# Counting some of a search's bounds on ScalarE with sums of signs, and one search no longer on TensorE

## The chip, the cores and the metric

The kernel runs on one core of a Trainium2 chip. The metric is the device time of one execution in microseconds (us), the median of several runs. Before the change it is 3851.02 us, the median of 3 runs from 3850.89 to 3852.55.

The engines of a core run side by side, each with its own instructions in order: TensorE (PE: matmuls; PEld: its weight loads), VectorE (DVE), ScalarE (ACT), GpSimd (POOL) and SyncE (SP), which here only issues transfers.

## The reference

The input is 8 sequences of 3072 tokens with 256 numbers each. Three parts follow each other.

1. The real part of a Fourier transform over the sequence and over the 256 numbers gives 24576 tokens of 256 numbers.
2. A layer of 8 experts. Each token has one score per expert (`x @ w_gate`). All 196608 pairs of token and expert are taken in order of falling score. A pair is skipped when its token already has an expert, or when its expert is full: each takes exactly 24576 / 8 = 3072 tokens. Then every token goes through its expert, `relu(x @ w1[e]) @ w2[e]`, with 1024 numbers in the middle.
3. A layer for all tokens, `h = x @ w_in` (2048 numbers), `g = max(h, 0) + alpha * min(h, 0)`, and `g @ w_out`.

## The kernel before

**Stages.** `fft_phase` computes the transform with matmuls and the scores `LG` (to about 410 us); `Router.first` finds the first expert that fills up and the list of its tokens, while TensorE has little else to do (to about 450 us). From there `ffn_phase` works through 48 tiles of 512 tokens, six tiles for each expert (`TPE`). The order of experts is that in which they fill up, so a next expert and its list have to be found while the tiles of an earlier one are computed.

**A tile.** For a tile `t`, i goes from 0 to 7 and each i has six parts: `l1` (the expert's first layer, six matmuls of 512 columns), `l3` (the first layer of part 3 for tile t-1), `l4` (its second layer, twelve matmuls of 256 columns), `l3`, `l2` (the expert's second layer) and `l4`. All numbers of a product are split into a high and a low half, and three products are summed. After the matmuls of a part are issued, one piece of background work is issued (`next(bg)`), and then the part's `evac()`: for `l1` ScalarE makes `hs` from PSUM and VectorE its low half; for `l3` ScalarE makes `r` and `a`, VectorE combines them, and ScalarE and VectorE make the halves of `g`, one `l3` later. The tiles of PSUM for `l1` and `l3` turn over three buffers.

**The background.** `background()` goes through the experts one after another with `router.round`, where n is the number of experts that are still open: 7, 6, ... 1. Every `yield` ends a piece; `lag()` yields until two further pieces have begun. A round has these steps: `rank` gives each token its best open expert (`aw`, and one-hot masks `ohe`); a search finds the score at which the first of the n experts is full; `choose` and `place` make the list of its tokens, with small matmuls in groups of 16, each after two pieces that VectorE prepares; then scores are moved for the next round. A round r (of 1 to 7) may begin at the tile (r-2)*6, and the list must be there when the last tile of the expert before is at i = 5: where it isn't, the pieces that are left are issued one after another with no layers between them.

**The search.** A token's key has two halves of 16 bits, searched one after the other. With n from 6 to 2, `search()` inside `round` finds 16 bits in 8 steps of 2 bits. `ke` holds the keys, masked for each expert. In each step VectorE counts, for every expert and each of three bounds, how many keys of a row reach the bound: a `tensor_scalar` with `accum_out` (L857). A matmul with ones (`total`, L848) sums the counts over the 128 rows, and VectorE compares the largest with the capacity, subtracts what was found from `ke`, and adds it to `base` (L867 to L874). With n below 6 each expert is a piece, with 6 two experts are; then come two pieces of `lag`, one for the matmul and one for the comparison.

With n = 7 the search is another one, `search_beside`: 4 bits a step, so 4 steps for each half. VectorE writes for each key which of 15 bounds it reaches (L725), and TensorE counts with 24 products a step (L735), 8 at a time, and a sum over the rows (L765). It runs from about 495 to 651 us.

Of the kernel before, what the change touches and what calls it, by code (L numbers as in the profile page):

```python
# [10 lines left out]
F32 = mybir.dt.float32  # L11
F32R = mybir.dt.float32r
BF16 = mybir.dt.bfloat16
I32 = mybir.dt.int32
I16 = mybir.dt.int16
U16 = mybir.dt.uint16
F16 = mybir.dt.float16
AF = mybir.ActivationFunctionType
ALU = mybir.AluOpType
AX = mybir.AxisListType  # L20
# [3 lines left out]
P = 128  # L24
B, N, D = 8, 3072, 256
E = 8
TOK = B * N
N1, N2 = 96, 32
NG = 24
# [239 lines left out]
class Router:  # L269
# [20 lines left out]
    def __init__(self, ctx, tc, LG):  # L290
# [12 lines left out]
        self.ohe = self.oh.rearrange("p a e -> p (a e)").rearrange("p (e a) -> p e a", e=E)  # L303
        self.eid = rp.tile([P, E], F32, name="eid")
        self.wm = rp.tile([P, 1], F32, name="wm")
        self.estar = rp.tile([P, 1], F32, name="estar")
        V.memset(self.done, 0.0)

# [381 lines left out]
                yield  # L690
        yield

    def search_beside(self, psum, n):


        nc, wp, V = self.nc, self.wp, self.nc.vector
        cap = self.CAP - 8 * 1536
        ke = wp.tile([P, E - 1, NCOL], U16, tag="ke", name="lows")
        kf = ke.rearrange("p e a -> p (e a)")
        lows = kf.bitcast(I16)[:, :512].rearrange("p (i k j) -> p i k j", i=4, j=8)  # L700
        dm = kf.bitcast(F32)[:, 256 : 256 + 8 * E].rearrange("p (e c) -> p e c", e=E)
        s2 = kf.bitcast(F16)[:, 640 : 640 + 16 * E].rearrange("p (e k) -> p e k", e=E)
        for i in range(4):
            nc.gpsimd.iota(lows[:, i], pattern=[[1 << 4 * i, 16], [0, 8]], base=-32768, channel_multiplier=0)
        H = NG // 3

        def blocks(t):
            return t.rearrange("p (a b) -> p a b", b=8)

        def search(key, exact=None):  # L710
            for i in reversed(range(4)):
                step = 1 << 4 * i
                last = exact is not None and i == 0
                k = 16 if last else 15
                first = 1 if last else 0
                q = 8 * k
                inds = {}

                def ind(h):
                    t = wp.tile([P, H, 16, 8], BF16, tag="ol", bufs=2, name="ind")  # L720
                    s = slice(h * H, h * H + H)
                    if last:
                        V.tensor_scalar(t[:, :, 0, :], blocks(exact)[:, s], self.base, None, op0=ALU.is_ge)
                    sh = [P, H, k - first, 8]
                    V.tensor_tensor(  # L725
                        t[:, :, first:k], blocks(key)[:, s, None, :].broadcast_to(sh),
                        lows[:, i, None, 16 - k + first :, :].broadcast_to(sh), op=ALU.is_ge,
                    )
                    inds[h] = t

                def products(h):
                    t = inds.pop(h)
                    for c in range(H):
                        a = (h * H + c) * 8
                        nc.tensor.matmul(  # L735
                            dv, t[:, c, :k].rearrange("p k j -> p (k j)"), self.ohe[:, :n, a : a + 8],
                            start=(h + c == 0), stop=(h == 2 and c == H - 1),
                        )

                ind(0)  # L740
                yield
                ind(1)
                yield from self.lag()
                d = psum(name="d")
                dv = d[:q, : 8 * n].rearrange("p (e c) -> p e c", e=n)
                products(0)
                yield
                ind(2)
                products(1)
                yield  # L750
                yield from self.lag()
                products(2)
                yield
                V.tensor_tensor(dm[:q, :n], dv, self.mske[:q, None, :].broadcast_to([q, n, 8]), op=ALU.mult)
                s = wp.tile([P, E], F32, tag="we", name="se")
                V.tensor_reduce(out=s[:q, :n], in_=dm[:q, :n], op=ALU.add, axis=AX.X)

                V.scalar_tensor_tensor(
                    s2[:q, :n, :k], s[:q, :n, None].broadcast_to([q, n, k]), -1536.0,
                    self.mskj[:q, None, :k].broadcast_to([q, n, k]), op0=ALU.add, op1=ALU.mult,  # L760
                )
                yield from self.lag()
                cnt = psum(name="cnt")
                cv = cnt[:, : n * k].rearrange("p (e k) -> p e k", e=n)
                nc.tensor.matmul(cv, self.ones[:q], s2[:q, :n, :k], start=True, stop=True)  # L765
                yield
                if last:
                    return cv
                mc = wp.tile([P, 16], F32, tag="mc", name="mc")
                V.tensor_reduce(out=mc[:, :k], in_=cv.rearrange("p e k -> p k e"), op=ALU.max, axis=AX.X)  # L770
                st = wp.tile([P, 16], F32, tag="st", name="st")
                V.memset(st[:, :k], float(step))
                nk = wp.tile([P, 1], F32, tag="nk", name="nk")
                V.scalar_tensor_tensor(
                    mc[:, :k], mc[:, :k], cap, st[:, :k], op0=ALU.is_ge, op1=ALU.mult, accum_out=nk
                )
                if i:
                    nxt = wp.tile([P, NCOL], I16, tag="cur", bufs=2, name="cur")
                    V.tensor_scalar(nxt, key, nk, -32768.0, op0=ALU.subtract, op1=ALU.max)
                    key = nxt  # L780
                V.tensor_tensor(self.base, self.base, nk, op=ALU.add)
                yield

        k16 = wp.tile([P, NCOL], I16, tag="k16b", name="k16b")
        V.tensor_scalar(k16, self.hi, -32768.0, None, op0=ALU.max)
        V.memset(self.base, -32768.0)
        yield
        yield from search(k16)
        key = self.low_key()
        V.tensor_scalar(k16, key, -32768.0, 32767.0, op0=ALU.max, op1=ALU.min)  # L790
        V.memset(self.base, -32768.0)
        yield
        cv = yield from search(k16, key)

        ce = wp.tile([P, E, 16], F32, tag="q1", name="ce")
        V.tensor_scalar(ce[:, :n], cv, cap, None, op0=ALU.is_ge)
        ne = wp.tile([P, E], F32, tag="ne", name="ne")
        V.tensor_reduce(out=ne[:, :n], in_=ce[:, :n], op=ALU.add, axis=AX.X)
        me = wp.tile([P, 1], F32, tag="me", name="me")
        V.tensor_reduce(out=me, in_=ne[:, :n], op=ALU.max, axis=AX.X)  # L800
        yield
        we = wp.tile([P, E], F32, tag="we", name="we")
        V.scalar_tensor_tensor(we[:, :n], ne[:, :n], me, self.wE[:, :n], op0=ALU.is_equal, op1=ALU.mult)
        V.scalar_tensor_tensor(self.base, me, -1.0, self.base, op0=ALU.add, op1=ALU.add)
        V.tensor_reduce(out=self.wm, in_=we[:, :n], op=ALU.max, axis=AX.X)
        V.scalar_tensor_tensor(
            we[:, :n], we[:, :n], self.wm, self.eid[:, :n], op0=ALU.is_equal, op1=ALU.mult, accum_out=self.estar
        )
        yield
        return key  # L810

    def round(self, psum, lists, n):

        nc, wp = self.nc, self.wp
# [7 lines left out]
            yield from self.place(psum, lists, at, n)  # L822
            return
        yield from self.rank(n)
        if n == E - 1:
            key = yield from self.search_beside(psum, n)
            at = self.choose(key)
            yield "expert"
            yield from self.place(psum, lists, at, n)
            return  # L830
        ke = wp.tile([P, E - 1, NCOL], U16, tag="ke", name="ke")
        s = wp.tile([P, E - 1, 3], BF16, tag="s", name="s")
        junk = [wp.tile([P, NCOL], BF16, tag="w", bufs=2, name="junk") for _ in range(2)]

        def keys(k16):
# [15 lines left out]
        def search():  # L851
            step = 65536
            while step > 1:
                step >>= 2
                for e in range(n):
                    for k in range(3):
                        V.tensor_scalar(  # L857
                            junk[(e + k) % 2], ke[:, e], float((k + 1) * step), 0.0, op0=ALU.is_ge, op1=ALU.add,
                            accum_out=s[:, e, k : k + 1],
                        )  # L860
                    if e % 2 or n < 6:
                        yield
                yield from self.lag()
# [1 line left out]
                yield  # L865
                mc = wp.tile([P, 3], F32, tag="mc", name="mc")
                V.tensor_reduce(out=mc, in_=cv.rearrange("p e k -> p k e"), op=ALU.max, axis=AX.X)  # L867
                st = wp.tile([P, 3], F32, tag="st", name="st")
                V.memset(st, float(step))
                nk = wp.tile([P, 1], F32, tag="nk", name="nk")  # L870
                V.scalar_tensor_tensor(mc, mc, self.CAP, st, op0=ALU.is_ge, op1=ALU.mult, accum_out=nk)
                if step > 1:
                    V.tensor_scalar(ke[:, :n], ke[:, :n], nk, 0.0, op0=ALU.subtract, op1=ALU.max)
                V.tensor_tensor(self.base, self.base, nk, op=ALU.add)  # L874
# [483 lines left out]
```

## Time and profile before

| | |
|---|---|
| median of 3 runs | 3851.02 us |
| the profiled execution | 3841.81 us, of which its span from first to last instruction is 3839.5 us |
| TensorE busy | 3789.3 us, 99% of the span |
| TensorE's weight loads | 3334.7 us, 87% |
| VectorE busy | 2522.5 us, 66% |
| ScalarE busy | 1818.2 us, 47% |
| GpSimd busy | 567.6 us, 15% |
| granted TensorE clock | 0.994 of full on average |

A share of busy time is an average over stages. TensorE is busy nearly throughout; where it is not, a list of its waits says for whom. The time from one instruction's start to the start of the next one on the same engine is often less than the duration of the first, since neighbours overlap.

### The profile page before, as it was taken

The page shows a single profiled execution, that of the slowest core. Times are in us where ns is not written, and L with a number is a line of the kernel's source. Part 1 is how long each engine was busy: PE and PEld are TensorE (multiplying, and loading weights), DVE is VectorE, ACT ScalarE, POOL GpSimd, SP SyncE. Part 2 cuts the span into 40 slices and gives each one's busy share as a digit, 9 for nine tenths or more (in the row PEclk, how much of TensorE's full clock was granted, in tenths as well). Part 3 has the DMA queues.
Part 4 walks back from the last instruction along what each step waited for, and adds up shares of the span by engine and source line. Part 5 has one row for each costly group of instructions (what it writes and reads, how often), then busy time and mean ns, then how long its engine had stood idle before and what let it go on. Part 6 is the DMA issues. An engine that isn't in the chain of part 4 may idle for free.

```text
span 3839.5 us, 61990 instructions
## 1 busy us (share of the span) xinstructions
PE 3789.3 (99%) x23859; PEld 3334.7 (87%) x23859; DVE 2522.5 (66%) x7024; ACT 1818.2 (47%) x3455; POOL 567.6 (15%) x845
## 2 busy tenths in 40 slices
PE   9999899999999999999999999999999999999999
PEld 8998588888888888888888888888888888888888
DVE  5776766688778876887677776677544444444444
ACT  4554244444445544454445444444545545554444
POOL 2121200020011110020111110110111101111010
PEclk9999899999999999999999999999999999999999
DMA  9776200010000000010001000010001000100000
GB/s 235 196 214 177 87 12 12 6 45 12 12 19 27 23 23 12 12 45 12 12 23 34 20 15 12 25 31 12 19 16 34 23 12 23 31 20 17 12 17 12
DMA packets 95048, 153.50 MB, mean 40 GB/s; under 512 B 14688, under 2 KB 64544, under 8 KB 94752
## 3 DMA queue, kind: packets, MB, share of 16 engines
q0 software_dynamic: 30400, 90.21, 7.9%
q1 hardware_dynamic: 63440, 58.75, 5.5%
q8 instruction: 187, 3.06, 0.3%
q14 instruction: 109, 0.89, 0.1%
q10 hardware_dynamic: 912, 0.58, 0.1%
HBM read 90.77 MB, written 58.72 MB: 39 GB/s over the span
## 4 chain that ended last, share of the span: by engine, by line
PE 92%; DVE 3%; issue 3%; DMA 1%; POOL 1%; ACT 1%; SPq 0%; POOLq 0%; ACTq 0%; DVEq 0%
PE o L1123 27%; PE u L1043 26%; PE y L1043 13%; PE h L1043 13%; PE b L209 4%; PE a L150 3%; PE ls L659 2%; PE c L226 2%; DVE junk L857 2%; PE xps L1033 1%; DMA x<-in_x 1%; DVE r L1096 1%; DVE g L1101 0%; PE d L735 0%; DMA rawx<-in_wcat,wi 0%
## 5 line engine op out<-in xcount | busy, mean ns | idle before, releaser
L1123 PEld LDWEIGHTS o<-w3t,g 128*128 128x128 f32 x9216 | 1178.3, 188 | 69.6 <-DVE g L1101 9.1
L1123 PE MATMUL o<-w3t,g 128*128 128x256 f32 x9216 | 1204.3, 280 | 8.5 <-DVE g L1101 6.8
L1043 PE MATMUL u<-ys,w3t 128*128 128x512 f32 x4608 | 1181.2, 393 | 0.2 <-DVE ys L1079 0.2
L1096 DVE SCALAR_TENSOR_TENSOR r<-a,nal,r 128x512 f32<-128x512 f32 x768 | 576.8, 751 | 638.8 <-ACT a L1095 636.0
L1043 PEld LDWEIGHTS u<-ys,w3t 128*128 128x128 f32 x4608 | 837.7, 188 | 158.1 <-DVE ys L1079 1.2
L1094 ACT ACTIVATE r<-u 128x512 f32<-128x512 f32 x768 | 459.6, 598 | 807.9 <-PE u L1043 680.0
L1056 ACT ACTIVATE hs<-h 128x512 fp32r<-128x512 f32 x384 | 230.4, 600 | 765.5 <-PE h L1043 731.1
L1146 POOL DMA_INDIRECT out_dram<-os,orow x192 | 190.7, 993 | 2624.8 <-ACT os L1142 2556.6
L1101 DVE TENSOR_TENSOR g<-r,g 128x512 fp32r<-128x512 f32 x768 | 526.3, 685 | 4.2
L1057 DVE SCALAR_TENSOR_TENSOR hs<-h,hs 128x512 fp32r<-128x512 f32 x384 | 264.9, 690 | 397.4 <-ACT hs L1056 396.6
L1043 PE MATMUL y<-hs,wxh 128*128 128x512 f32 x1536 | 491.2, 401 | 1.3 <-DVE hs L1057 1.2
L1100 ACT CAST g<-r 128x512 fp32r<-128x512 f32 x768 | 478.3, 623 | 20.7 <-DVE r L1096 20.6
L1095 ACT ACTIVATE a<-u 128x512 f32<-128x512 f32 x768 | 454.9, 592 | 0.0
L1043 PEld LDWEIGHTS y<-hs,wxh 128*128 128x128 f32 x1536 | 283.0, 189 | 62.1 <-DVE hs L1057 2.2
L1043 PE MATMUL h<-xth,wxh 128*128 128x512 f32 x768 | 303.4, 395 | 0.2
L1043 PE MATMUL y<-hs,wxl 128*128 128x512 f32 x768 | 303.6, 395 | 0.0
L1043 PE MATMUL h<-xtl,wxh 128*128 128x512 f32 x768 | 300.6, 391 | 0.2 <-DVE xtl L1038 0.2
L1043 PE MATMUL h<-xth,wxl 128*128 128x512 f32 x768 | 299.5, 390 | 0.0
L857 DVE TENSOR_SCALAR_CACHE_REDUCE junk<-ke 128x192 bf16<-128x192 uint16 x960 | 276.1, 348 | 0.1
L1017 POOL DMA_INDIRECT xg<-XD,idx x192 | 211.0, 1099 | 94.7 <-issue 55.5
L1043 PEld LDWEIGHTS y<-hs,wxl 128*128 128x128 f32 x768 | 144.2, 188 | 35.0
L1043 PEld LDWEIGHTS h<-xth,wxl 128*128 128x128 f32 x768 | 144.2, 188 | 32.1
(257 smaller groups left out, 3577.3 us busy)
## 6 DMA issues: line engine op xcount, KB each, us to landing
x<-in_x SPq DMA_DIRECT2D x63, 384.0 KB, 4.6
XD<-xs SPq DMA_DIRECT2D x96, 128.0 KB, 2.9
XD<-xs SPq DMA_DIRECT2D x184, 64.0 KB, 2.7
raw<-in_w POOLq DMA_DIRECT2D x32, 256.0 KB, 4.4
W3S<-hl POOLq DMA_DIRECT2D x32, 256.0 KB, 3.1
w3t<-W3S SPq DMA_DIRECT2D x16, 512.0 KB, 9.8
tw<-in_tw POOLq DMA_DIRECT2D x12, 512.0 KB, 6.3
xg<-XD,idx POOLq DMA_INDIRECT x192, 2.8
```

What stands on the lines that cost most here:

```text
L857: V.tensor_scalar(junk[(e + k) % 2], ke[:, e], float((k + 1) * step), 0.0, op0=ALU.is_ge, op1=ALU.add, accum_out=s[:, e, k : k + 1],)
L1017: nc.gpsimd.indirect_dma_start(out=x[:, j, :], out_offset=None, in_=XD, in_offset=bass.IndirectOffsetOnAxis(ap=idx[:, j0 + j : j0 + j + 1] ...
L1043: nc.tensor.matmul(o, w, a, start=(first and n == 0), stop=(last and n == 2))
L1056: nc.scalar.activation(h[:, 0], ps, AF.Relu)
L1057: nc.vector.scalar_tensor_tensor(h[:, 1], ps, 0.0, h[:, 0].bitcast(F32), op0=ALU.max, op1=ALU.subtract)
L1094: nc.scalar.activation(r, ps, AF.Relu)
L1095: nc.scalar.activation(a, ps, AF.Relu, scale=-1.0)
L1096: nc.vector.scalar_tensor_tensor(r, a, nal[:, j : j + 1], r, op0=ALU.mult, op1=ALU.add)
L1100: nc.scalar.copy(g[:, 0], r)
L1101: nc.vector.tensor_sub(g[:, 1], r, g[:, 0].bitcast(F32))
L1123: nc.tensor.matmul(o[:, s, :], a, w, start=(j == 0 and n == 0 and s % 2 == 0), stop=(j == 15 and n == 2 and s % 2 == 1), skip_group_check= ...
L1146: ins = nc.gpsimd.indirect_dma_start(out=out, out_offset=bass.IndirectOffsetOnAxis(ap=orow[:, jj : jj + 1], axis=0), in_=os[:, s, :], in_o ...
```

## The change

Two things change. The search with n = 7 is done by `search()` like the others, and `search_beside` is gone; so its steps have 2 bits instead of 4, and TensorE only sums over the rows. And in `search()` VectorE counts only `own` of the three bounds, 1 where n is 7 and 2 otherwise. For the other bounds ScalarE takes the sign of key minus bound plus a half for each key, and sums the signs of a row with `accum_out`: keys that reach the bound give 1, others -1, so that a sum over all tokens of 2 * capacity - tokens or more means that the bound is reached by enough. `bounds` holds the offsets as per-partition operands and `caps` the limits, 26 small memsets at the very start; the comparison has two instructions on VectorE as before, without a memset of its own.

```diff
@@ Router.__init__
+        self.bounds = rp.tile([P, 24], F32, name="bounds")
+        self.caps = rp.tile([P, 6], F32, name="caps")
+        for i in range(8):
+            for k in range(3):
+                V.memset(self.bounds[:, 3 * i + k : 3 * i + k + 1], 0.5 - (k + 1) * 4**i)
+        V.memset(self.caps[:, :3], self.CAP)
+        V.memset(self.caps[:, 3:], 2 * self.CAP - TOK)
...
-    def search_beside(self, psum, n):
...
@@ Router.round
         yield from self.rank(n)
-        if n == E - 1:
-            key = yield from self.search_beside(psum, n)
-            at = self.choose(key)
-            yield "expert"
-            yield from self.place(psum, lists, at, n)
-            return
         ke = wp.tile([P, E - 1, NCOL], U16, tag="ke", name="ke")
         s = wp.tile([P, E - 1, 3], BF16, tag="s", name="s")
+
+        own = 1 if n == E - 1 else 2
+        junk2 = wp.tile([P, NCOL], BF16, tag="ae", name="junk2")
...
             while step > 1:
                 step >>= 2
+                i = step.bit_length() // 2
                 for e in range(n):
                     for k in range(3):
-                        V.tensor_scalar(
-                            junk[(e + k) % 2], ke[:, e], float((k + 1) * step), 0.0, op0=ALU.is_ge, op1=ALU.add,
-                            accum_out=s[:, e, k : k + 1],
-                        )
+                        if k < own:
+                            V.tensor_scalar(
+                                junk[(e + k) % 2], ke[:, e], float((k + 1) * step), 0.0, op0=ALU.is_ge, op1=ALU.add,
+                                accum_out=s[:, e, k : k + 1],
+                            )
+                        else:
+
+                            with nc.allow_low_precision(reason="whole numbers up to 192"):
+                                nc.scalar.activation(
+                                    junk2, ke[:, e], AF.Sign, bias=self.bounds[:, 3 * i + k : 3 * i + k + 1],
+                                    accum_out=s[:, e, k : k + 1],
+                                )
                     if e % 2 or n < 6:
                         yield
...
                 V.tensor_reduce(out=mc, in_=cv.rearrange("p e k -> p k e"), op=ALU.max, axis=AX.X)
-                st = wp.tile([P, 3], F32, tag="st", name="st")
-                V.memset(st, float(step))
                 nk = wp.tile([P, 1], F32, tag="nk", name="nk")
-                V.scalar_tensor_tensor(mc, mc, self.CAP, st, op0=ALU.is_ge, op1=ALU.mult, accum_out=nk)
+                V.tensor_tensor(mc, mc, self.caps[:, 3 - own : 6 - own], op=ALU.is_ge)
+                V.tensor_scalar(mc, mc, float(step), 0.0, op0=ALU.mult, op1=ALU.add, accum_out=nk)
```

## Rows read from the trace of the kernel before

**Rows 1.** Stretches: us, their length, busy us (x instructions) by engine, clock, DMA.
```profile
core 0: us, PE busy (x) PEld busy (x) DVE busy (x) ACT busy (x) POOL busy (x), PEclk, DMA share, GB/s
500.00:651.00 151.00, 151.00 (x1004) 131.11 (x1003) 87.48 (x189) 68.28 (x126) 17.96 (x24) 1.00 0.05 15
818.00:1022.00 204.00, 194.56 (x1104) 165.56 (x1103) 180.34 (x824) 93.89 (x173) 28.30 (x40) 0.99 0.06 19
```

**Rows 2.** TensorE's waits, 800 to 1030 us: us in total, times, longest.
```profile
PE o L1123 <- DVE g L1101: 5.7, 5, 1.7
PE cnt L848 <- DVE junk L857: 3.5, 8, 1.3
```

**Rows 3.** The chain of waits, 490 to 530 us: start, us, what.
```profile
496.01 1.37 PE h L1043 x6
...
498.75 1.40 PE o L1123 x12
500.15 0.41 PE d L735 x8
500.56 1.47 PE u L1043 x6
...
510.00 1.38 PE u L1043 x6
511.38 0.07 PE cnt L765
```

**Rows 4.** Groups by line: busy us, mean ns of one | idle before.
```profile
L735 PE MATMUL d<-oh,ind 128*120 128x56 bf16 (+1 forms) x192 | 13.2, 209 | 0.0
L869 DVE MEMSET st<- 128x3 f32 x80 | 4.9, 61 | 0.0
```

**Rows 5.** VectorE in order of time, 818 to 834 us: start, us, what.
```profile
818.60 0.35 DVE L857 TENSOR_SCALAR_CACHE_REDUCE junk<-ke 128x192 bf16<-128x192 uint16 x1
818.87 0.09 DVE L857 DVE_READ_ACCUMULATOR junk<-ke 128x1 bf16 x1
818.87 0.35 DVE L857 TENSOR_SCALAR_CACHE_REDUCE junk<-ke 128x192 bf16<-128x192 uint16 x1
...
824.11 0.69 DVE L1057 SCALAR_TENSOR_TENSOR hs<-h,hs 128x512 fp32r<-128x512 f32 x1
824.71 0.75 DVE L1096 SCALAR_TENSOR_TENSOR r<-a,nal,r 128x512 f32<-128x512 f32 x1
825.37 0.69 DVE L1101 TENSOR_TENSOR g<-r,g 128x512 fp32r<-128x512 f32 x1
...
828.55 0.17 DVE L867 TENSOR_REDUCE mc<-cnt 128x3 f32<-128x18 f32 x1
...
829.53 0.35 DVE L857 TENSOR_SCALAR_CACHE_REDUCE junk<-ke 128x192 bf16<-128x192 uint16 x1
```

**Rows 6.** ScalarE in order of time, the same stretch.
```profile
826.16 0.60 ACT L1094 ACTIVATE r<-u 128x512 f32<-128x512 f32 x1 [3.00 <-DVE g L1101]
826.65 0.59 ACT L1095 ACTIVATE a<-u 128x512 f32<-128x512 f32 x1
827.13 0.62 ACT L1100 CAST g<-r 128x512 fp32r<-128x512 f32 x1
827.64 0.63 ACT L945 CAST wxh<-rawx 128x512 fp32r<-128x512 f32 x1
```

**Rows 7.** Groups by line, ScalarE: busy us, mean ns of one | idle before.
```profile
L211 ACT CAST yh<-b 128x276 fp32r<-128x276 f32 x192 | 74.7, 390 | 57.6 <-PE b L209 54.2 <-DVE b L105 1.4 <-DVE q L391 0.6
L1100 ACT CAST g<-r 128x512 fp32r<-128x512 f32 x768 | 478.3, 623 | 20.7 <-DVE r L1096 20.6
L625 ACT ACTIVATE rr<-eq,pf 128x1152 bf16<-128x1152 bf16 x4 | 5.0, 1254 | 19.3 <-DVE eq L620 19.3
L157 ACT ACT_TABLE_LOAD x1 | 1.3, 1283 | 2.2 <-issue 2.2
```

**Rows 8.** The second list's end on VectorE, and the transfer that needs it.
```profile
774.42 0.18 DVE L584 SCALAR_TENSOR_TENSOR idx<-lm 128x24 int32<-128x24 f32 x1
...
814.46 1.03 POOL L1017 DMA_INDIRECT xg<-XD,idx x1 [0.30 <-issue]
```

**Rows 9.** The program's first 12 us in order of time: VectorE's first evacuation.
```profile
7.33 0.56 DVE L158 TENSOR_TENSOR ul<-a,uh 128x384 fp32r<-128x384 f32 x1 [3.88 <-ACT uh L157]
```

More of the change, by code (lines that the diff above doesn't have):

```diff
@@ L691, in rank @@
         yield
-    def search_beside(self, psum, n):
[L696 to L727, printed above, removed]
-                    )
[L729 to L810, printed above, removed]
@@ L854, in search @@
                 step >>= 2
+                i = step.bit_length() // 2
                 for e in range(n):
                     for k in range(3):
-                        V.tensor_scalar(
-                            junk[(e + k) % 2], ke[:, e], float((k + 1) * step), 0.0, op0=ALU.is_ge, op1=ALU.add,
-                            accum_out=s[:, e, k : k + 1],
-                        )
+                        if k < own:
[9 more added lines that the diff above has]
+                                )
                     if e % 2 or n < 6:
```

## The prediction

> **What bounds the kernel now.** I read the stretches first: for each, the busy time of every engine [rows 1]. In the seven experts' search (500 to 651 us) TensorE is busy for the whole stretch, and ScalarE for 68 of 151 us: every TensorE instruction taken away there shortens the run, and the other engines have room. In the six experts' search (818 to 1022 us) TensorE lacks 9.4 of 204 us while VectorE is busy for 180: the one place behind the opening where TensorE waits. TensorE's waits there name the cause [rows 2]: 5.7 us for a half `g` in L1101 and 3.5 us for the last count in L857, both VectorE. The chain of waits gives the price of a TensorE instruction between the layers [rows 3], the timelines of VectorE and ScalarE the time from one instruction's start to the next one's, which is what an engine in order really pays [rows 5, 6].
>
> I call one call of `next(bg)` a beat. TensorE works 1.37 to 1.40 us for a layer, so for a beat [rows 3].
>
> **Part 1: the products go.** Eight products hold TensorE 0.41 us and the six layer matmuls behind them take 1.47 instead of 1.38 [rows 3]: 0.50 us a group. 192 products [rows 4] are 24 groups: -12.0 us. Counts: 8 of 0.07 us go [rows 3], and 17 come (16 steps and the last compare); at the same price +0.6 us.
>
> **Part 2: relief in the six experts' search.** A step there has 18 counts on VectorE. A count takes 0.35 us, and its accumulator read 0.09, but starts are 0.27 apart [rows 5]: 4.9 us. In the 7 beats of a step (3 bunches, 2 of lag, 1 for the count, 1 for the reduction) VectorE also evacuates: 0.60 for `hs`, 0.66 for `r`, about 0.6 for `g`, so 3.1 us in six beats and 3.6 in seven, and 0.98 us for the reduction chain from L867 to the next count [rows 5]. Together 9.5 of 9.8 us: that is why TensorE waits. With 12 counts it is 7.9. ScalarE gets 6 signs beside 4.1 us of evacuation (below): 6.8 us at most 7.5. Neither is the bound any more, so the 9.2 us of [rows 2] go. From none to all of it is possible; I take all, as each wait there ends on VectorE. For five experts and fewer there are no waits to remove, and one sign a beat fits.
>
> **Part 3: the price of a sign.** No row shows Sign or an accumulating activation. Casts: 276 columns take 390 ns, 512 take 623, and 1152 with a per-partition scale 1254 [rows 7]. On the line through 598 ns for 512 columns from PSUM (0.60 in [rows 6]) and 390 for 276, a column costs 0.88 ns and an empty instruction 0.15 us. So 192 columns from SBUF cost 0.34, and the per-partition operand adds about 0.07 (1254 against 623 + 640 x 0.88): 0.41 us. Starts of neighbours lie 0.11 us closer than that: `r` takes 0.60, but `a` starts 0.49 later [rows 6]. The sum must then be read out. If the read hides as VectorE's does [rows 5], a sign costs 0.30; if nothing overlaps, 0.41 + 0.15 = 0.56. I take 0.45, one overlap of the two, nearest to the middle, since ScalarE's empty instruction is longer than VectorE's read of 0.09.
>
> The Trainium skill, "ScalarE: Activation LUTs", section "What ACT_TABLE_LOAD costs", gives 280 ns + 0.833 per column with a pointer bias and an overlap of 93 ns, so, as an estimate, 0.35 us from start to start; it has no price for the read. By it alone rival A would hold; [rows 6] agree with the overlap (0.11).
>
> **Part 4: what the signs do to the seven experts' search.** A step now has 14 signs and 7 counts. ScalarE's evacuation is 0.49 for `hs` and 0.49 + 0.48 + 0.51 for each of two `r`, `a`, `g` [rows 6]: 3.5 us in six beats, 4.1 in seven; with 14 x 0.45 = 6.3 it is 10.4 us, above TensorE's 9.8. And the steps form a loop: the count needs the last sign, the next step's signs need `ke` after that count. From the count's start: the first sign waits for ScalarE to evacuate the layer behind the count (its products end 1.6 us after, plus its evacuation), and for VectorE's chain of 0.98 us, which stands behind the evacuation of the layer ahead of the count. By which layer that is (l1, l3, l4, l3, l2, l4) the first sign starts 3.2, 3.7, 3.2, 3.7, 1.7 or 2.2 us after the count, mean 2.95. Between the four bunches of signs ScalarE does three evacuations: 1.5, 1.5, 0.5, 2.0, 2.0 or 3.0 us, mean 1.75. With 0.2 for the last sign's result that is 4.9 us. The loop needs 14 x sign + 4.9 against 7 beats and the count, 9.8. So TensorE waits for 14 x sign - 4.9 us in each of 16 steps: nothing at 0.35 us a sign, 1.4 us at 0.45, so +22.4 us. What is queued behind the signs on ScalarE is the evacuation of the same beat; where it makes `g` or `hs` late, TensorE waits in L1123 or L1043 too. In [rows 2] such waits were larger than those of the count; here the wait at the count lets ScalarE catch up, and I put 5 us (1 to 10).
>
> **Part 5: the list comes late.** By its yields the old search lasts 99 beats, the new 128 (2 and 2 for keys, 16 x 7, 1, 7 + 2 + 1 + 1 for the last compare). The second list stood at beat 197 and is needed at beat 222: in the trace 774.4 and 814.5 us [rows 8], 40 us for 25 beats. It now stands at beat 226, and four calls run without layers between them: two of lag, the last 16 placing matmuls, the copies. TensorE finds VectorE's last pieces not ready and has no layer to cover them: +2.3 us (1 to 4). The expert is known at beat 157 and needed at 195. The later rounds come 29 beats later too; counted in the same way, the third list still has 46 beats to spare and those behind it more.
>
> **Nothing** for the 26 memsets at the start: about 0.06 us each [rows 4], 1.6 us, and VectorE sits idle for 3.88 us before its first evacuation [rows 9]. The two instructions in the reduction replace two.
>
> **Sum.** -12.0 + 0.6 - 9.2 + 22.4 + 5 + 2.3 = +9 us. The profiled execution took 3841.8 us (span 3839.5, 2.3 around it), 9.2 less than the median 3851.0 of the three timed runs; I put the difference on the median: 3860. Without parts 3 and 4 it would be -18 us; a sign's price moves it by 224 counts, so 2.2 us for each 10 ns. That is the whole question.
>
> **Rivals.**
> A. The read hides, a sign costs 0.30 to 0.36: no more than 3 us of waits in the seven experts' search, so -18.3 + 3 = -15 us, 3836. For it: VectorE's reads cost nothing [rows 5]. Against: the loop must then close within 9.8 us in every phase, and three of the six phases are longer than the mean.
> B. 0.36 to 0.43 us: waits of 2 to 18 us and the 5 of the layers cancel the gain: 3851 within 8.
> C. Nothing overlaps, 0.56 us: 16 x 2.9 = 47 of waits, 8 behind layers, 2 for the list, -20.6: +37 us, 3888. Waits of 3 us and more could also drop the granted clock, as in the stretch of [rows 1] with the waits, whose mean is 0.99, not 1.00, of the upper level. It decides from 0.52 us a sign up.
> D. Sign needs other tables. One load of 1.28 us stands in the whole trace [rows 7]. The Trainium skill, the same page, section "Table sets: the hidden batching unit", says that functions load in named sets and that cheap ones like relu are in every set; a set with Sign would then serve all, and the change costs at most a load or two. Were there a load at each turn from Sign to Relu and back, 336 bunches (64 + 48 + 224) would bring 672 loads of 1.28 us, 860 us on ScalarE; the bunches of the seven experts alone, 64 x 2.6 = 164 us, would nearly all be waits: above 4000 us.
>
> **Chances.** Forecast (0.43 to 0.52, slower by 5 to 28 us) 0.40; A 0.22; B 0.20; C 0.15; D 0.03. About 0.2%, 7.7 us, can be told from no change. Forecast runs below that bound count as the same: faster 0.22, same 0.25, slower 0.53. The range goes from A to C, 3836 to 3890.
>
> **What would show it.** The start-to-start time of the signs with their reads, the first thing to read. A row TensorE count <- ScalarE of some 20 us in the seven experts' search, its stretch some 75 us longer, 46 of it the 29 beats. In the six experts' search no wait for L857. No product of L735. A wait of the placing matmuls near the second list. Wrong if TensorE is full in both searches (A), or if VectorE's chain, not ScalarE, ends the count's wait.

## The result

The changed kernel takes 3889.83 us, the median of 5 runs (3889.36 to 3896.84), against 3851.02 of the kernel before beside it: 38.8 us more, a ratio of 1.0105 with a 95% interval from 1.0094 to 1.0117. It is slower, as forecast, inside the range, but by four times the 9 us of the forecast. Times of the kernel before differ from one chip to the next (3851 us here; 3841, 3838 and 3839 below), so runs are compared by their ratios to the kernel before on the same chip.

The page of the changed kernel, the costliest groups by line, with the columns of [rows 4]. The sign is L753, VectorE's count L746:

```profile
span 3887.5 us, 62440 instructions
...
PE 3794.5 (98%) x23666; PEld 3333.9 (86%) x23676; DVE 2492.4 (64%) x6652; ACT 2078.7 (53%) x4543; POOL 571.7 (15%) x841
...
L753 ACT ACTIVATE junk<-ke,bounds 128x192 bf16<-128x192 uint16 x544 | 248.1, 456 | 108.1 <-DVE ke L768 66.8
...
L746 DVE TENSOR_SCALAR_CACHE_REDUCE junk<-ke 128x192 bf16<-128x192 uint16 x752 | 232.4, 348 | 4.2
```

There are 224 signs for seven experts and 320 for the others. TensorE's waits in the seven experts' search, 470 to 760 us, answer to [rows 2]:

```profile
PE cnt L735 <- ACT junk L753: 27.3, 12, 3.4
PE cnt L735 <- DVE junk L746: 9.0, 2, 5.4
PE o L1018 <- DVE g L996: 2.3, 7, 0.4
PE h L938 <- DVE hs L952: 1.3, 2, 0.8
```

The two waits put down to VectorE's count do end on VectorE, but ScalarE made it late. At 525.98 us the last sign's read had ended 0.27 us before and VectorE's last read 0.14 us before; that count of VectorE's stands behind an evacuation which waited 3.55 us for `a`, and on ScalarE `a` stands behind the signs. The second such wait, at 717.11 us, has the same order.

```profile
524.21 0.75 DVE L991 SCALAR_TENSOR_TENSOR r<-a,nal,r 128x512 f32<-128x512 f32 x1 [3.55 <-ACT a L990]
525.52 0.19 ACT L753 ACTIVATION_READ_ACCUMULATOR junk<-ke,bounds 128x1 bf16 x1
525.75 0.09 DVE L746 DVE_READ_ACCUMULATOR junk<-ke 128x1 bf16 x1
525.98 0.18 PE L735 MATMUL cnt<-s,onesb 128*128 128x21 bf16 x1 [3.56 <-DVE junk L746]
```

The 16 steps of the search lie in the second to fourth tile, from one tile's finished `ys` to another's. The stretches, columns as in [rows 1]: the opening, these three tiles, the rest without the last 57 us; first of before, then of the changed kernel:

```profile
474.50:690.80 216.30, 216.07 (x1398) 187.42 (x1398) 136.70 (x304) 99.15 (x183) 20.91 (x28) 1.00 0.04 13
690.80:3782.30 3091.50, 3081.77 (x18711) 2694.73 (x18711) 2023.83 (x5706) 1489.10 (x2745) 437.00 (x576) 1.00 0.07 20
```

```profile
0.00:479.50 479.50, 440.63 (x3433) 408.09 (x3444) 338.49 (x1005) 201.33 (x475) 100.20 (x222) 0.95 0.65 181
479.50:741.20 261.70, 221.40 (x1170) 186.79 (x1170) 150.37 (x505) 213.09 (x630) 20.79 (x28) 0.93 0.04 11
741.20:3830.20 3089.00, 3083.66 (x18756) 2695.70 (x18756) 1978.84 (x5107) 1636.23 (x3385) 441.74 (x576) 1.00 0.07 20
```

The three tiles grew by 45.4 us: TensorE lacks 40.3 us there, and the granted clock averages 0.93 where it was 1.00, so about a seventh of the time at the lower level, 1.2 GHz. The rest is 2.5 us shorter, and 6 in a second pair of traces (e5, e6). 44 small matmuls that place the second list were in the three tiles before and now come behind them, so the rest keeps less than the relief of the six experts' search. The opening, 474.5 us before, grew by 5.0; the experiments show that it differs by more than that between executions.

Here is the sign, ScalarE in order of time (start, us, what):

```profile
522.07 0.46 ACT L753 ACTIVATE junk<-ke,bounds 128x192 bf16<-128x192 uint16 x1
522.44 0.19 ACT L753 ACTIVATION_READ_ACCUMULATOR junk<-ke,bounds 128x1 bf16 x1
522.66 0.46 ACT L753 ACTIVATE junk<-ke,bounds 128x192 bf16<-128x192 uint16 x1
523.02 0.19 ACT L753 ACTIVATION_READ_ACCUMULATOR junk<-ke,bounds 128x1 bf16 x1
523.11 0.57 ACT L989 ACTIVATE r<-u 128x512 f32<-128x512 f32 x1
```

From sign to sign are 0.58 to 0.59 us; the forecast had 0.45, and 0.56 as its upper end. From the start of a read to the next sign are 0.22 us, so that sign starts 0.03 us after the read's end; from the start of a read to an evacuation are 0.09.

### The profile page after: what moved, and what is told of

Same layout as the page of the kernel before. It is cut to its first block, busy times and chain, and to the rows that moved or that the text cites. A ratio compares the mean times of both kernels' runs of the same rounds, so it can differ in the third digit from the quotient of the medians.

```text
span 3887.5 us, 62440 instructions
## 1 busy us (share of the span) xinstructions
PE 3794.5 (98%) x23666; PEld 3333.9 (86%) x23676; DVE 2492.4 (64%) x6652; ACT 2078.7 (53%) x4543; POOL 571.7 (15%) x841
## 4 chain that ended last, share of the span: by engine, by line
PE 85%; ACT 6%; DVE 4%; issue 3%; DMA 1%; POOL 1%; another core or an unknown queue 0%; SPq 0%; POOLq 0%; ACTq 0%; DVEq 0%
PE o L1018 25%; PE u L938 24%; PE y L938 12%; PE h L938 12%; PE b L209 3%; ACT junk L753 3%; PE a L150 3%; PE ls L668 2%; PE c L226 2%; DVE r L991 1%; PE xps L928 1%; DMA x<-in_x 1%; DVE g L996 1%; ACT r L989 1%; ACT a L990 1%
## 5 line engine op out<-in xcount | busy, mean ns | idle before, releaser
L753 ACT ACTIVATE junk<-ke,bounds 128x192 bf16<-128x192 uint16 x544 | 248.1, 456 | 108.1 <-DVE ke L768 66.8
L746 DVE TENSOR_SCALAR_CACHE_REDUCE junk<-ke 128x192 bf16<-128x192 uint16 x752 | 232.4, 348 | 4.2
```

Of the source, the lines that this page charges most:

```text
L746: V.tensor_scalar(junk[(e + k) % 2], ke[:, e], float((k + 1) * step), 0.0, op0=ALU.is_ge, op1=ALU.add, accum_out=s[:, e, k : k + 1],)
L753: nc.scalar.activation(junk2, ke[:, e], AF.Sign, bias=self.bounds[:, 3 * i + k : 3 * i + k + 1], accum_out=s[:, e, k : k + 1],)
```

## The experiments

Theory P: the price of a sign closes ScalarE's loop later than TensorE's work. Its rivals: L, the loop of two-bit steps as such; C, TensorE's clock. Of P's price: W, each sign waits for the scratch tile that the one before writes; R, a sum waits for the read of the one before.

**Two counts for VectorE, one for ScalarE** (e1)

```diff
-        own = 1 if n == E - 1 else 2
+        own = 2
```

> The changed kernel with one difference: in the seven experts' search VectorE counts two of the three bounds and ScalarE one, as for fewer experts. Theory P (the price of a sign: 0.58 us from start to start, so that 14 signs close ScalarE's loop at 14 x 0.58 + 4.9 = 13.0 us against 9.8 of TensorE's work): with 7 signs the loop needs 9.0 us, VectorE 3.8 + 3.6 + 1.0 = 8.4, and at most 5 us of waits for the count are left: some 3836 us, 15 below the kernel before. Theory L (it is the loop of 16 two-bit steps that TensorE waits for, each with a count, VectorE's comparison and new keys, whoever counts): over 30 us of waits stay and it takes over 3870. Theory C (it is the TensorE clock that fell in this search): waits go as in P, and the stretch shows no half clock.

Measured: 0.9965 of before (0.9952 to 0.9979), 3827.5 us: 13.7 less. TensorE's waits from 470 to 1100 us, the largest, and the three tiles:

```profile
PE cnt L735 <- DVE junk L746: 2.7, 6, 1.4
PE cnt L735 <- ACT a L990: 1.5, 4, 0.5
...
477.30:685.50 208.20, 203.75 (x1171) 175.39 (x1171) 185.57 (x729) 152.65 (x407) 20.54 (x28) 1.00 0.04 14
```

The three tiles take 208.2 us, 8.1 less than before, and TensorE is busy for 203.8 of them. The loop of 16 steps is the same and nearly all waits are gone: L falls.

**All three counts on VectorE** (e2)

```diff
-        own = 1 if n == E - 1 else 2
+        own = 3 if n == E - 1 else 2
```

> The changed kernel, but all three bounds of the seven experts' search are counted by VectorE; the rounds of fewer experts keep their signs. P: ScalarE has nothing of it, but VectorE now needs 21 x 0.273 + 3.6 + 1.0 = 10.4 us in a step against 9.8: 10 to 20 us of waits, all ending on VectorE; about 3848 us. L: as with the two counts, over 3870.

Measured: 0.9993 (0.9984 to 1.0002); waits for L746 of 11.7 us, three tiles of 221.2. As P has it: then VectorE is too slow for a step, but not by much.

**The old search for seven experts, signs for fewer** (e3): `search_beside` and its call back in place.

> The changed kernel with the kernel before's search of the seven experts (products on TensorE); signs only in the rounds of six experts and fewer. P: the 9.2 us of waits in the six experts' search go and nothing else changes: 3842 to 3845 us. If the signs of later rounds cost what the relief gives: 3851, and the tiles from the sixth on take as long as before.

Measured: 0.9970 (0.9958 to 0.9982), 12.9 us less. The eight tiles with the six experts' search, first before, then here:

```profile
768.80:1343.30 574.50, 565.06 (x3386) 488.99 (x3385) 473.00 (x1773) 274.01 (x505) 86.26 (x112) 1.00 0.08 23
```

```profile
764.30:1328.50 564.20, 562.15 (x3386) 487.29 (x3386) 445.90 (x1464) 347.60 (x816) 85.07 (x112) 1.00 0.08 23
```

10.3 us less, with the same matmuls. The signs of the later rounds take nothing of the forecast gain. By itself each part's gain is there (e1 for the first search); the loss comes with the seven experts' 224 signs.

**Small matmuls in the wait** (e4)

```diff
+            if n == E - 1:
+                for _ in range(14):
+                    nc.tensor.matmul(cnt[:, 256:512], self.tri, ..., start=True, stop=True)
             nc.tensor.matmul(cv, self.onesb[:, :P], s[:, :n, :k], start=True, stop=True)
```

> The changed kernel with 14 small matmuls ahead of each count of the seven experts' search, into columns of its PSUM tile that nobody reads: they keep TensorE at work in about 1.5 us of each wait. Theory P (ScalarE's loop alone sets the time, and TensorE's half clock only fills time that it would wait in): time as the changed kernel, 3890 within 4, with less half clock and with idle time in its place. Theory C (the half clock costs on top, 34 us of it, so up to 17): 3873 to 3880.

Measured: 1.0100 (1.0084 to 1.0115), the ratio of the changed kernel. The three tiles:

```profile
470.60:733.40 262.80, 236.99 (x1394) 200.24 (x1393) 150.53 (x505) 212.98 (x631) 20.86 (x28) 0.98 0.04 11
```

262.8 us against 261.7, with a clock of 0.98 instead of 0.93. The idle time fell from 40.3 to 25.8 us, since the added matmuls fill it; I had expected it to rise. The length stays, but not because the lower clock cost nothing. From count to count, step by step, four steps are 0.4 to 1.3 us shorter than in the changed kernel, 2.9 us together, and three are 0.9 to 1.5 us longer, 3.8 together. The layer behind the second count, in the changed kernel and here, and the added matmuls ahead of the fifth count:

```profile
526.00 2.90 PE L938 MATMUL u<-ys,w3t 128*128 128x512 f32 x6
...
516.99 1.64 PE L943 MATMUL u<-ys,w3t 128*128 128x512 f32 x6
...
561.58 1.70 PE L737 MATMUL cnt<-oh,tri 128*128 128x256 bf16 x14
563.12 0.17 PE L740 MATMUL cnt<-s,onesb 128*128 128x21 bf16 x1
```

Where that layer takes 1.64 us instead of 2.90, ScalarE evacuates it earlier, and the first sign starts 3.2 us after the count instead of 4.5. The longer steps are the added matmuls' own: the last sign's read had ended at 560.33. So the lower clock costs some 3 us of the 45, and nothing that shows in the other steps, where it uses up time in which TensorE would wait. As the cause of the loss C falls; at 0.98 a little of its cost may remain.

**Two signs more in a step** (e7): each with its sum into a spare column.

```diff
+                    if n == E - 1 and e in (1, 3):
...
+                            nc.scalar.activation(
+                                junk2, ke[:, e], AF.Sign, ...
+                                accum_out=self.spare[:, e : e + 1],
+                            )
```

> The changed kernel with two more signs in each step of the seven experts' search, 16 instead of 14, whose sums nobody reads. Theory P (ScalarE's loop sets the time of a step: signs x 0.583 + 4.9 us): 32 signs more, +18.7 us over the changed kernel, all of it in the three tiles of that search. If the count waits for something beside ScalarE's signs (VectorE's counts, its comparison), clearly less than that: under 8 us.

Measured: 1.0161 (1.0144 to 1.0178), 3898.3 us, beside 3878.7 of the changed kernel on the same chip: 19.6 more. The three tiles:

```profile
470.30:751.30 281.00, 229.92 (x1171) 193.26 (x1170) 150.80 (x505) 230.72 (x695) 20.80 (x28) 0.91 0.03 10
```

281.0 us, 19.5 more than in e5: 0.61 us for each of the 32 signs.

**The changed kernel again** (e5) and **the kernel before again** (e6)

> The changed kernel once more, beside the others on one chip: 1.010 of the kernel before. Its first tile took 7.5 us longer than in the trace of the kernel before, by one wait of 9.6 us on ScalarE that no instruction ends. If that belongs to the change it stands in this trace too; if it belongs to the execution, it is gone, and the opening takes 470 to 475 us.

> The kernel before, for a second trace of it: the opening to the first finished tile took 474.5 us. If the opening differs by several us from one execution to another, it does so here, with the same instructions, and nothing of it is the change's.

Measured: 1.0102 (1.0085 to 1.0119) for the changed kernel, its opening 475.7 us and the wait gone; the kernel before once 3837.7 us, its opening 470.4. These two differ by 5.3 us, as the first two traces did by 5.0, so they alone don't settle it. But e4 and e7, which have the changed kernel's instructions up to there, have openings of 470.6 and 470.3, shorter than the 474.5 of the kernel before: the opening differs by up to 9 us between executions of the same work. In the first trace of the changed kernel the wait made the first tile, from its first `xth` to its first `ys`, 7.5 us longer (34.3 against 26.8; 26.5 in e5). What ScalarE waited for there stays open. The three tiles were 261.5 us again, and 216.4; from the first finished tile to the end the changed kernel takes 39.1 us more here (3404.0 against 3364.9).

**Prices of an activation** (e8): 32 activations whose results nobody reads, in the opening of e1's kernel.

> The kernel with two counts and one sign, and in its opening, where ScalarE waits for about 26 us, 32 activations of the same 128 x 192 tile whose results nobody reads: five Signs each with bias operand and sum, with the operand alone, with the sum alone, with neither; three pairs of a Sign with sum and one without; three pairs of a Sign with sum and a Relu. Theory R (a sum makes the next sum wait for its read): from start to start 0.58, 0.36, 0.51 and 0.29 us, and a pair takes 0.45 + 0.36 = 0.81, not 0.58 + 0.36. Theory S (Sign itself or the per-partition operand is dear): the operand alone is over 0.45, and the sum adds less than 0.1.

Measured: with operand and sum 0.58; operand alone 2.43 for five, 0.49; sum alone 0.49; neither 1.98 for five, 0.40; a pair of a Sign with sum and one without 1.07, of a Sign with sum and a Relu 0.98. ScalarE in order of time; x5 stands for five:

```profile
368.68 0.45 ACT L530 ACTIVATE po<-k,bounds 128x192 bf16<-128x192 uint16 x1
369.04 0.19 ACT L530 ACTIVATION_READ_ACCUMULATOR po<-k,bounds 128x1 bf16 x1
369.26 2.40 ACT L532 ACTIVATE po<-k,bounds 128x192 bf16<-128x192 uint16 x5
371.69 0.36 ACT L534 ACTIVATE po<-k 128x192 bf16<-128x192 uint16 x1
...
374.14 1.94 ACT L536 ACTIVATE po<-k 128x192 bf16<-128x192 uint16 x5
376.12 0.45 ACT L538 ACTIVATE po<-k,bounds 128x192 bf16<-128x192 uint16 x1
...
379.90 0.36 ACT L542 ACTIVATE po<-k 128x192 bf16<-128x192 uint16 x1
380.30 0.45 ACT L541 ACTIVATE po<-k,bounds 128x192 bf16<-128x192 uint16 x1
```

Theory R's prices without a sum fail: 0.49 and 0.40 us, where it had 0.36 and 0.29. Theory S's two numbers come out, but not its cause: the Relu (L542) takes 0.40 as Sign does, so Sign is not dear, and the operand adds 0.09, the sum 0.09 to 0.10. Even with neither, 0.40 us pass from start to start for 0.36 of work, where [rows 6] have neighbours overlap by 0.11. In all four forms the next one starts 0.03 us after the one before, with its read, has ended, and the trace has each of them wait on a semaphore that ScalarE's instruction before it raises. All write one tile, `po` here and `junk2` in the change; `r`, `a` and `g` of [rows 6] write three. So the program may have each sign wait for the one before since it writes what that wrote; the next run tests it.

**Three scratch tiles in turn** (e9), of space that the search does not use:

```diff
         junk2 = wp.tile([P, NCOL], BF16, tag="ae", name="junk2")
+        more = wp.tile([P, 2, NCOL], BF16, tag="at", name="more")
+        outs = (junk2, more[:, 0], more[:, 1])
...
+                                turn[0] += 1
                                 nc.scalar.activation(
-                                    junk2, ke[:, e], AF.Sign, ...
+                                    outs[turn[0] % 3], ke[:, e], AF.Sign, ...
```

> The changed kernel in which the signs write three scratch tiles in turn instead of one (the values of a sign are used by nobody, only its sum). In the run of prices an activation with neither sum nor operand took 0.40 us from start to start, though it lasts 0.36, and each waited for the one before, as they write one tile; the sum added 0.10. Theory W (each sign waits until the one before has written the same tile): without that wait a sign costs 0.36 to its read and 0.09 to 0.10 for it, 0.46 in all; the loop of a step is 14 x 0.46 + 4.9 = 11.3 us, TensorE waits 1.5 us a step instead of 3.3, and it takes 28 us less than the changed kernel: 1.003 of the kernel before. Theory R (the next sum waits for the read of the one before, whatever it writes): 0.58 us stay, and 1.010.

Measured: 1.0026 (1.0017 to 1.0035), 3850.1 us: 11.2 over before, where the changed kernel is 39 to 41 over. ScalarE:

```profile
522.48 0.45 ACT L757 ACTIVATE junk<-ke,bounds 128x192 bf16<-128x192 uint16 x1
522.83 0.20 ACT L757 ACTIVATION_READ_ACCUMULATOR junk<-ke,bounds 128x1 bf16 x1
522.92 0.45 ACT L757 ACTIVATE more<-ke,bounds 128x192 bf16<-128x192 uint16 x1
523.26 0.20 ACT L757 ACTIVATION_READ_ACCUMULATOR more<-ke,bounds 128x1 bf16 x1
523.36 0.45 ACT L757 ACTIVATE more<-ke,bounds 128x192 bf16<-128x192 uint16 x1
...
475.40:709.90 234.50, 210.32 (x1170) 178.31 (x1170) 150.97 (x505) 192.19 (x630) 20.02 (x28) 0.99 0.04 12
```

A sign starts 0.44 us after the one before and 0.09 after that one's read has started, while the read still runs. The three tiles (last line) take 234.5 us. W holds, R falls: the read holds the next sign up only where that sign writes the same tile.

**Two counts and three scratch tiles** (e10), and **the list in time** (e11: two experts a piece in the last compare)

> Two counts on VectorE and one sign for all rounds, with three scratch tiles in turn. ScalarE was no bound with two counts (0.9965 of the kernel before), so W and R expect the same but for the last us or two of waits: 0.9955 to 0.9965.

> As the kernel with two counts and three scratch tiles, and in the last compare of the seven and the six experts' search two experts are one piece, so that the second list comes 4 beats earlier, in time for the transfer. Were the late list worth the 2.3 us that were forecast, 0.9950 to 0.9960; the trace of the changed kernel showed one wait of 0.7 us there, so no more than 1 us is expected: 0.9953 to 0.9963, the same within the interval.

Measured: 0.9953 (0.9939 to 0.9967), 3820.1 us, and 0.9958 (0.9945 to 0.9972). Both are faster than either kernel; between them, and from e1, no difference can be told by these times. The traces, one each, hint at one: from the first finished tile to the end e1 takes 3350.7 us (3350.8 in e8, the same kernel there), e10 3346.5, and 2.5 of the 4.2 us lie in three tiles of the six experts' search (209.8 and 207.3 us). So the one scratch tile costs a little there too. The late list is worth too little to show: e11 takes 3347.8.

## Why the prediction went wrong

**The step that failed** is part 3, the price of a sign: "I take 0.45, one overlap of the two". It is 0.583, over the 0.56 where nothing overlaps. I took the overlap of 0.11 from `r`, `a` and `g` [rows 6], which write three tiles, and did not see that 14 signs in a row write one. The change adds a wait of each sign for the one before, and the prediction has no such wait: 0.36 us to the read, 0.19 for it and 0.03 to the next sign. With three tiles the sign costs 0.44, and the kernel is 0.26% over before, 10.0 us, where 9 were forecast. That both come so near is partly luck: the sign lasts 0.46 where 0.41 was forecast, and its read adds 0.09 instead of 0.15; and the other terms below are off by some 1 to 3 us each and nearly cancel.

The terms one by one, in the three tiles beside the 203.8 us of TensorE's work in e1, which has the same instructions on TensorE there:

- The loop, 16 x (signs x price - 4.9) + 5, gives 57.2 us at 14 x 0.583 and 75.8 at 16 x 0.583; lost were 57.9 and 77.2 (e7). At 14 x 0.44 it gives 25.2, and 30.7 were lost (e9). Its form was right; the forecast's 22.4 + 5 is near the loss of e9, not that of the change.
- The products: forecast were -12.0 + 0.6 = -11.4 us. e1's three tiles are 8.1 us shorter than before with 4.5 of idle time, but 44 placing matmuls have left them too. e3 differs from e1 in this search alone: from the first finished tile to the end e1 takes 3350.7 us against 3354.9, 4.2 less, so with its 4.5 of idle time the products gave some 9 us, less what the late list costs.
- The relief of the six experts' search: 9.2 forecast, 10.3 in e3.
- The late list: 2.3 forecast; the trace of the changed kernel has one wait of 0.7 us for it, and e11 gains nothing that can be told.
- The memsets and the tables: one table load stands in the whole trace of the changed kernel as before [rows 7], so rival D is out. The Trainium skill's statement ("ScalarE: Activation LUTs", section "Table sets: the hidden batching unit") that cheap functions like relu stand in every set agrees with it; it does not name Sign there.

Of the prediction's rivals C came nearest in time, with 37 us; its cause, that nothing overlaps, holds, but as a wait on a scratch tile, and the lower clock that it named cost some 3 us (e4). A failed even without that wait: the read is short but not hidden, 0.09 us from start to start, and the sign itself is longer than forecast.

The Trainium skill, the same page, section "What ACT_TABLE_LOAD costs", has an overlap of 93 ns for neighbours and 93 ns for a pointer operand. The operand agrees (0.49 against 0.40 in e8). The overlap does where tiles differ (e9), and not where they are the same (e8).

## What to carry to other kernels

Before an engine is given many small instructions in a row, look at what each writes: a result that nobody needs still has a place, and one scratch tile for all strings them on a chain of waits, here 0.14 us for each of 224. A price from start to start holds only between instructions that share as little as those it was read from. And in a loop through several engines work out each one's round trip: with 14 signs a step the kernel is 39 us slower than before, with 7 it is 13.7 faster.

## What the runs showed of the hardware

A sum on ScalarE is a second instruction of 0.19 us; the next activation, where it writes another tile, starts 0.09 us after that one's start (e9). VectorE's read of 0.09 starts together with the next count [rows 5]. Where TensorE waited 2 to 3 us in most steps, the granted clock averaged 0.93, about a seventh of the time at 1.2 GHz; while ScalarE set the pace, that cost some 3 us of 262 (e4).
